# A decode kernel that streams its weights: half a row of w_q goes first, the keys second, and ACT's transfers begin behind a memset

## The chip, the cores and the metric

The kernel runs on one core of one Trainium2 chip. The metric is the device time of one execution in microseconds; the median of a few runs is given, with the lowest and the highest.

## The reference

One token (`x`, 576 numbers) goes through a sliding-window attention with cached keys and values and through a dense layer with gelu; a gate mixes the two.

```python
W = min(4096, max(256, Sk // 4))                      # the last 4096 positions of 32768
q = (x @ wq).reshape(B, Sq, Hq, Dh)                   # 32 query heads of 128
k = repeat(k_cache[:, :, Sk - W:, :], 2, axis=1)      # 16 heads of keys and values
v = repeat(v_cache[:, :, Sk - W:, :], 2, axis=1)
p = softmax(q . k * Dh ** -0.5)
a = (p . v).reshape(B, Sq, Hq * Dh) @ wo
b = gelu(x @ w1 + b1) @ w2 + b2                       # 576 -> 4608 -> 576
g = sigmoid((x * gate_w).sum(-1))
return g * a + (1 - g) * b
```

All arrays are bfloat16. Every byte of the windowed keys and values and of the weights is used once, which makes 53.6 MB to be read.

## The kernel before

**The order is written out by hand.** The kernel is under a manual schedule: each engine runs its instructions in the order in which the program states them. All large transfers are issued by SP in one queue of hardware DMA. ACT issues three small ones.

**The tiles.** Keys and values are loaded as eight tiles each of two heads (`load_kv`, its `dma_start` is line 102): 64 partitions for the one head, 64 for the other, and 16,384 bytes for each partition. Six buffers (`kv_pool`) hold them. `load_flat` (line 118, its `dma_start` is line 120) loads a flat stretch of w_q or w1 as 128 partitions; three buffers (`w_pool`) hold those. w_q comes as two tiles of 18,432 bytes per partition, `wq_t[0]` and `wq_t[1]`; a partition has four and a half rows of w_q, each 8,192 bytes long.

**The head of the program.** SP issues, in this order: the first keys (line 134), x9 (line 136, x as 64 x 9), the two w_q tiles, and the second keys (line 142). ACT issues x_row (line 130), gate_w (line 131) and b2 (line 132). b2 goes into row 0 of `b2_r`, a tile that GpSimd fills with zeros first (line 129), so its transfer waits for that memset; it is the third of ACT's, and b2 is used at the end of the kernel alone (line 679).

**What follows.** TensorE multiplies x9 with a selection matrix into `x_ps` (line 373); VectorE makes from it `x2`, the stationary operand of the w_q and w1 products (line 381). VectorE then multiplies x_row with gw_row (line 385), and TensorE spreads the sum over the partitions for the gate (line 390). Behind that product stand the transposes of the first two heads of keys (line 235, copied out by VectorE and ACT at lines 244 and 246), and then the 36 products with w_q (line 409), half of them on each tile of w_q. The scores (line 266) need q. A loop over the 16 heads then interleaves transposes, scores, the softmax of groups of four heads and the products with the values (line 342), with w1 placed among them (line 454). At the end come wo and w2 (line 671), the last quarter of w2 in three pieces (line 690), the copy of the result (line 703) and its transfer (line 704).

**Completion counters.** DMAs issued by SP and ACT take turns on eight completion counters. A DMA that takes a counter for the second time waits until the one that had it before has landed. In the built program before, the ninth DMA in this order is SP's third tile of keys, and it waits for one of ACT's small transfers.

Of the kernel before, what the change touches and what calls it, by code (L numbers as in the profile page):

```python
# [16 lines left out]
def kernel(  # L17
# [15 lines left out]
    nc = tc.nc  # L33
# [13 lines left out]
    NQ = 4  # L47
# [6 lines left out]
    NM = 9  # L54


    QC = Hq * Dh // 8
# [33 lines left out]
    wq_flat = A_wq.rearrange("a b -> (a b)").rearrange("(p n) -> p n", p=P)  # L91
# [7 lines left out]
    def load_kv(cache, m, name):  # L99
        t = kv_pool.tile([P, NCK, Dh], BF16, name=name, tag="kv")  # L100

        nc.sync.dma_start(  # L102
            out=t[:],
            in_=cache[0, 2 * m : 2 * m + 2, Sk - W : Sk, :].rearrange(
                "e (p c) d -> p e (c d)", c=NCK
            ),
        )
        return t

    def load_k(m):  # L110
        return load_kv(A_k_cache, m, "k_t")
# [3 lines left out]

    WMAX = 41 * 256

    def load_flat(src, lo, n, name):
        t = w_pool.tile([P, WMAX], BF16, name=name, tag="w")
        nc.sync.dma_start(out=t[:, 0:n], in_=src[:, lo : lo + n])  # L120
        return t

    k_tiles, v_tiles = {}, {}
# [3 lines left out]

    b2_r = const.tile([P, D], BF16, name="b2_r")
    nc.gpsimd.memset(b2_r[:], 0.0)
    nc.scalar.dma_start(out=x_row[:], in_=A_x.rearrange("a b d -> (a b) d"))  # L130
    nc.scalar.dma_start(out=gw_row[:], in_=gate_w.rearrange("(o n) -> o n", o=1))
    nc.scalar.dma_start(out=b2_r[0:1, :], in_=B_b2.rearrange("(o n) -> o n", o=1))

    k_tiles[0] = load_k(0)
    x9 = const.tile([P // 2, NM], BF16, name="x9")
    nc.sync.dma_start(out=x9[:], in_=A_x.rearrange("a b (i m) -> (a b i) m", m=NM))
    wq_t = []
    QP = 2 * NM
    for i in range(2):
        wq_t.append(load_flat(wq_flat, i * QP * QC, QP * QC, "wq_t"))  # L140

    k_tiles[1] = load_k(1)

# [12 lines left out]
        out=row_f[:], in_=ident_f[:, 0 : 32 * (NQ - 1) + 1 : 32], axis=AX.X, op=ALU.add  # L156
# [4 lines left out]
        out=dup[:].rearrange("k (i e) -> k i e", e=2),  # L161
        in_=ident[0 : P // 2, 0 : P // 2].rearrange("k (i e) -> k i e", e=1).to_broadcast(
            [P // 2, P // 2, 2]
        ),
    )
    par = const.tile([P, 2], FP32, name="par")
    for o in range(2):
        nc.vector.tensor_reduce(
            out=par[:, o : o + 1],
            in_=ident_f[:].rearrange("p (i o) -> p o i", o=2)[:, o, :],  # L170
# [7 lines left out]
        out=turn[:].rearrange("p j (h q) -> p j h q", h=OJ),  # L178
        in_=ident[:].rearrange("p (o q j) -> p j o q", o=1, j=OJ).to_broadcast(
            [P, OJ, OJ, P // OJ]  # L180
        ),
# [4 lines left out]
        out=m_r[:], in_=ident_f[:].rearrange("p (s r) -> p r s", r=R), axis=AX.X, op=ALU.add  # L186
# [5 lines left out]
        out=row_e[:], in_=ident_f[:].rearrange("p (a e q) -> p e a q", e=2, q=2), axis=AX.XY,  # L192
# [3 lines left out]
        out=row_e[:], in0=row_e[:], scalar1=-MASK, scalar2=MASK, op0=ALU.mult, op1=ALU.add  # L196
    )
    mask = const.tile([P, BC * P], BF16, name="mask")
    for e in range(2):
        nc.vector.tensor_copy(  # L200
            out=mask[:, e::2], in_=row_e[:, e : e + 1].to_broadcast([P, BC * P // 2])
# [4 lines left out]
        out=m_c[:], in_=ident_f[:].rearrange("p (t c r) -> p c t r", c=BC, r=R), axis=AX.XY,  # L206
# [4 lines left out]
        out=m_hl[:], in_=ident_f[:].rearrange("p (h q) -> p h q", h=OJ), axis=AX.X, op=ALU.add  # L211
# [10 lines left out]
    for dst, src in ((sel, ident), (sel_f, ident_f)):  # L222
        nc.vector.tensor_copy(
            out=dst[:].rearrange("p l (o h) -> p l o h", o=2),
            in_=src[:].rearrange("p (h l x) -> p l x h", h=2, l=2)[:, :, 0:2, :],
# [149 lines left out]
    for dst, src, s in (  # L375
# [10 lines left out]
        out=junk[:], in0=x_row[:], in1=gw_row[:], scale=1.0, scalar=0.0,  # L386
# [11 lines left out]
        out=omg[:], in0=g_t[:], scalar1=-1.0, scalar2=1.0, op0=ALU.mult, op1=ALU.add  # L398
# [7 lines left out]
    for b in range(NM * NQ):  # L406
        m, t = b // NQ, b % NQ
# [22 lines left out]
    for m in range(HB // 2):  # L430
        lo = R * (NGR - 1) + RP * m
        nc.vector.tensor_copy(  # L432
            out=qz[:, m :: HB // 2, lo : lo + RP],
            in_=qT[:, :, m, :].rearrange("p i b -> p b i"),
# [7 lines left out]
    def w1_load(i):  # L442
        return load_flat(w1_flat, i * W1N, W1N, "w1_t")
# [105 lines left out]
    for h in range(NU):  # L549
# [4 lines left out]
        if h == 1:  # L554

            for o in range(2):
                nc.sync.dma_start(
                    out=b1_r[o : o + 32 * (NQ - 1) + 1 : 32],
                    in_=B_b1.rearrange("(o t k n) -> o t k n", o=2, t=NQ, k=2)[o],
# [57 lines left out]
    for i in range(NOG // 2):  # L617
        t = w_pool.tile([P, WMAX], BF16, name="wo_t", tag="w")
        nc.sync.dma_start(
            out=t[:, 0 : 2 * OJ * D].rearrange("p (o n) -> p o n", o=2),  # L620
            in_=wo_view[:, 2 * i : 2 * i + 2, :],
# [3 lines left out]
    for g in range(NG):  # L625
        t = kv_pool.tile([P, NCK * Dh], BF16, name="w2_t", tag="kv")
# [7 lines left out]
        out=ot[:], in0=o_sb[:], scalar=g_t[:, 0:1], in1=r_sums[:], op0=ALU.mult, op1=ALU.mult  # L634
# [3 lines left out]
    for j in range(OJ):  # L638
# [3 lines left out]
        out=ow_m[:],  # L642
# [5 lines left out]
    with nc.allow_low_precision("one of the eight summands is not zero"):  # L648
        nc.vector.tensor_reduce(  # L649
            out=ow[:].rearrange("p j o -> p (j o)"), in_=ow_m[:], axis=AX.X, op=ALU.add  # L650
# [17 lines left out]
    for n, four in enumerate(blocks):  # L668
# [11 lines left out]
        out=part_s[:], in0=b2_r[:].rearrange("p (k n) -> p k n", k=2), scalar=omg[:, 0:1],  # L680
# [16 lines left out]
    for j in range(RJ):  # L697
# [7 lines left out]
        out=out.rearrange("a b (t n) -> (a b t) n", t=NQ), in_=y[0 : 32 * (NQ - 1) + 1 : 32, :]  # L705
# [31 lines left out]
```

## Time and profile before

| | |
|---|---|
| time, median of 3 runs | 134.98 us (134.93 to 135.19) |
| time of the profiled execution | 134.92 us |
| its span, first to last instruction | 133.0 us |
| PE busy | 90.9 us (68%) |
| DVE busy | 61.3 us (46%) |
| ACT busy | 48.5 us (36%) |
| POOL busy | 4.2 us (3%) |
| DMA packets, bytes | 4553 packets, 53.79 MB, mean 404 GB/s |

The profiled execution's time is 1.92 us longer than its span: what lies around the first and the last instruction. Times in the views are microseconds from the first instruction; in a timeline row come start, duration, engine, line, operation and, in brackets, how long the engine sat idle before it and what ended that. "SPq" and "ACTq" are the engines' queues issuing DMAs, and the duration is that of the issue, not of the transfer. A stretch of time lists its ends and its length, then for each engine its busy time and its number of instructions (PE, weight loads, DVE, ACT, POOL), then TensorE's granted clock, the share of the 16 DMA engines that was busy, and the bytes of the packets that start in it, as GB/s.

### The profile page before, as it was taken

Reading aid. Unit: us, or ns where it says so; the run is one execution under the profiler, and the core shown is the slowest. Engines: PE = TensorE matmul, PEld = TensorE weight load, DVE = VectorE, ACT = ScalarE, POOL = GpSimd, SP = SyncE. Lnnn points to the kernel's source line nnn. Section 1 sums busy time; section 2 is a strip of 40 time slices with the busy share of each in tenths; the row PEclk is TensorE's granted clock in tenths of the full one; section 3 lists DMA queues with packets and bytes.
Section 4 is the critical chain, followed back from the end, with each engine's and each line's share of the span. In section 5 each row is a group of like instructions: output and inputs, shape, how many; then the busy total and the mean of one; then the engine's idle time right before and its main releaser. Section 6 shows DMA issues by size and latency. Waiting matters only on the chain.

```text
span 133.0 us, 2659 instructions
## 1 busy us (share of the span) xinstructions
PE 90.9 (68%) x1127; PEld 58.6 (44%) x1127; DVE 61.3 (46%) x165; ACT 48.5 (36%) x91; POOL 4.2 (3%) x11
## 2 busy tenths in 40 slices
PE   0007985299296899969076996978988648459660
PEld 0007741267174565645045654645655215135340
DVE  4964632035227665575004257564866463440020
ACT  3003750066336787757001153766584100000000
POOL 8400000000000000000000000000000000000000
PEclk9999999757999999999955559999999955555865
DMA  3999999999999999999899999999999999999960
GB/s 79 400 430 432 443 424 429 434 436 412 431 458 399 453 414 446 409 421 479 379 453 409 448 414 443 419 439 424 434 429 429 415 418 430 436 424 415 428 261 0
DMA packets 4553, 53.79 MB, mean 404 GB/s; under 512 B 563, under 2 KB 702, under 8 KB 1214
## 3 DMA queue, kind: packets, MB, share of 16 engines
q1 hardware_dynamic: 4536, 53.62, 95.2%
q8 instruction: 9, 0.15, 0.4%
q14 instruction: 2, 0.02, 0.0%
q10 hardware_dynamic: 6, 0.00, 0.0%
HBM read 53.62 MB, written 0.00 MB: 403 GB/s over the span
## 4 chain that ended last, share of the span: by engine, by line
DMA 58%; PE 28%; DVE 8%; SPq 2%; issue 2%; DVEq 0%
DMA w_t<-in_B_w_dram 41%; DMA k_t<-in_A_k_cache_dram 17%; PE tp L235 13%; PE s_ps L266 4%; PE acc L342 3%; DVE kT L244 3%; PE h_ps L454 2%; PE hT L481 2%; DVE a_s L358 2%; PE y_ps L690 1%; SPq L120 1%; SPq L102 1%; DVE ez L320 1%; DVE part_s L679 1%; DVE h_r L472 1%
## 5 line engine op out<-in xcount | busy, mean ns | idle before, releaser
L246 ACT CAST kT<-tp 128x512 bf16<-128x512 f32 x80 | 44.1, 586 | 44.2 <-PE tp L235 43.7
L244 DVE CAST kT<-tp 128x512 bf16<-128x512 f32 x48 | 33.0, 690 | 38.6 <-PE tp L235 34.1
L235 PE MATMUL tp<-ident,k_t 128*128 128x128 bf16 x512 | 45.5, 238 | 4.7 <-DMA k_t<-in_A_k_cache_dram 3.0
L235 PEld LDWEIGHTS <-k_t 128*128 128x128 bf16 x512 | 35.2, 107 | 17.4 <-issue 12.8
L342 PE MATMUL acc<-v_t,ez 128*32 128x512 bf16 x128 | 13.3, 459 | 2.2 <-DVE a_s L358 1.9
L266 PE MATMUL s_ps<-kT,qz 128*32 128x512 bf16 x128 | 13.5, 416 | 0.3 <-DVE qz L432 0.3
L454 PE MATMUL h_ps<-w_t,x 128*32 128x288 bf16 x72 | 4.0, 365 | 6.8 <-DMA w_t<-in_B_w_dram 6.8
L454 PEld LDWEIGHTS <-x 128*32 128x32 bf16 x72 | 2.8, 117 | 7.6 <-issue 7.1
L373 PE MATMUL x_ps<-x,dup 64*128 64x9 bf16 x1 | 0.2, 163 | 8.8 <-DMA x<-in_A_x_dram 8.8
L342 PEld LDWEIGHTS <-ez 128*32 128x32 bf16 x128 | 3.7, 102 | 5.5 <-issue 3.1
L266 PEld LDWEIGHTS <-qz 128*32 128x32 bf16 x128 | 3.3, 94 | 3.8 <-issue 0.8
L679 DVE SCALAR_TENSOR_TENSOR part_s<-b_r,omg,part 128x576 f32<-128x576 bf16 x1 | 0.8, 814 | 8.8 <-PE part L671 8.8
L671 PE MATMUL part<-wo_t,ow 128*1 128x288 bf16 x64 | 4.0, 443 | 1.0 <-DVE ow L649 1.0
L671 PE MATMUL part<-w_t,gt 128*1 128x288 bf16 x54 | 3.7, 364 | 1.4 <-DMA w_t<-in_B_w_dram 1.4
L358 DVE SCALAR_TENSOR_TENSOR a_s<-acc,m_c,a_s 128x128 f32<-128x128 f32 x12 | 4.2, 351 | 0.4
L307 ACT ACTIVATE pr<-ms,nb 128x512 bf16<-128x512 f32 x4 | 2.9, 722 | 4.1 <-DVE nb L304 4.1
L320 DVE COPY ez<-pT 128x64 bf16<-128x64 bf16 x32 | 3.6, 183 | 1.7 <-PE pT L315 1.5
L148 DVE CAST ident_f<-ident 128x128 f32<-128x128 bf16 x1 | 3.0, 3000 | 1.8 <-POOL ident masks.py:199 1.8
L365 PE MATMUL o_ps<-m_r,a_s 128*128 128x8 f32 x8 | 1.9, 315 | 2.8 <-DVE a_s L358 2.8
L365 PEld LDWEIGHTS o_ps<-m_r,a_s 128*128 128x128 f32 x8 | 1.6, 249 | 4.9 <-DVE a_s L358 2.5
L671 PEld LDWEIGHTS <-gt 128*1 128x1 bf16 x54 | 2.2, 104 | 2.9 <-issue 2.0
L481 PE MATMUL hT<-sel_f,h_r 128*64 128x4 f32 x36 | 2.7, 264 | 1.2 <-DVE h_r L472 1.2
(82 smaller groups left out, 48.2 us busy)
## 6 DMA issues: line engine op xcount, KB each, us to landing
k_t<-in_A_k_cache_dram SPq DMA_DIRECT2D x8, 2048.0 KB, 27.5
v_t<-in_A_v_cache_dram SPq DMA_DIRECT2D x8, 2048.0 KB, 24.5
w_t<-in_B_w_dram SPq DMA_DIRECT2D x2, 2592.0 KB
wq_t<-in_A_wq_dram SPq DMA_DIRECT2D x2, 2304.0 KB, 14.4
wo_t<-in_A_wo_dram SPq DMA_DIRECT2D x2, 2304.0 KB
w_t<-in_B_w_dram SPq DMA_DIRECT2D x2, 1296.0 KB, 21.6
w_t<-in_B_w_dram SPq DMA_DIRECT2D x1, 864.0 KB
w_t<-in_B_w_dram SPq DMA_DIRECT2D x1, 720.0 KB, 21.3
```

Of the source, the lines that this page charges most:

```text
L148: nc.vector.tensor_copy(out=ident_f[:], in_=ident[:])
L235: nc.tensor.matmul(tp[:, c * P : (c + 1) * P], lhsT=k_tiles[h // 2][:, (h % 2) * NCH + i * BC + c, :], rhs=ident[:], start=True, stop=True,)
L244: nc.vector.tensor_copy(out=dst, in_=tp[:])
L246: nc.scalar.copy(out=dst, in_=tp[:])
L266: nc.tensor.matmul(s_tiles[b][32 * t : 32 * (t + 1), :], lhsT=qz[:, h // 2, lo : lo + 32], rhs=kT[h][:, i * BC * P : (i + 1) * BC * P], st ...
L320: nc.vector.tensor_copy(out=ez[:, b % 2, m, NQ * s : NQ * (s + 1), :, RP * m : RP * (m + 1)], in_=pT[:].rearrange("p c (t s r) -> p t c s ...
L342: nc.tensor.matmul(acc[b][32 * ct : 32 * ct + 4 * R, :, :], lhsT=ez[:, b % 2, ul // 2, n, :, :].rearrange("p c r -> p (c r)"), rhs=v_tiles ...
L358: nc.vector.scalar_tensor_tensor(out=a_s[:], in0=acc[b][:, c, :], scalar=m_c[:, c : c + 1], in1=a_s[:], op0=ALU.mult, op1=ALU.add,)
L365: nc.tensor.matmul(o_ps[:], lhsT=a_s[:], rhs=m_r[:], start=True, stop=True)
L454: nc.tensor.matmul(h_box[0][32 * t : 32 * (t + 1), k, 0:FB], lhsT=x2[:, m, :], rhs=w[:, off : off + FB], start=(m == 0), stop=(m == NM - 1),)
L481: nc.tensor.matmul(box[0][64 * e : 64 * (e + 1), j, :], lhsT=rows[:, j : j + RJ * 63 + 1 : RJ], rhs=sel_f[:, e, :], start=True, stop=True,)
L671: nc.tensor.matmul(part[32 * t : 32 * t + 1, k, 0:DB], lhsT=col, rhs=w[:, i * D + k * DB : i * D + (k + 1) * DB], start=(n == 0), stop=(n ...
```

## The change

`load_flat` gets cuts: a stretch may come in several transfers, and a function given as `between` is called after the first. The first tile of w_q is cut after 2,048 elements, so its first transfer is 4,096 bytes for each of 128 partitions, half a row of w_q. It becomes the first transfer that SP issues; then come the first keys and x9, then the other 14,336 bytes per partition of the same tile, the second w_q tile and the second keys, as before. SP issues one DMA more.

On ACT, b2's transfer, which waits for the memset of `b2_r`, moves from the third place to the first; x_row and gate_w follow it.

In the built program the ninth DMA in the order of the completion counters is now SP's second tile of keys, and it waits for b2's. No instruction of PE, DVE or POOL is added, removed or moved.

```diff
-    def load_flat(src, lo, n, name):
+    def load_flat(src, lo, n, name, cuts=(), between=None):
         t = w_pool.tile([P, WMAX], BF16, name=name, tag="w")
-        nc.sync.dma_start(out=t[:, 0:n], in_=src[:, lo : lo + n])
+        edges = (0, *cuts, n)
+        for i, (a, b) in enumerate(zip(edges, edges[1:])):
+            if i == 1 and between is not None:
+                between()
+            nc.sync.dma_start(out=t[:, a:b], in_=src[:, lo + a : lo + b])
         return t
...
     nc.gpsimd.memset(b2_r[:], 0.0)
+    nc.scalar.dma_start(out=b2_r[0:1, :], in_=B_b2.rearrange("(o n) -> o n", o=1))
     nc.scalar.dma_start(out=x_row[:], in_=A_x.rearrange("a b d -> (a b) d"))
     nc.scalar.dma_start(out=gw_row[:], in_=gate_w.rearrange("(o n) -> o n", o=1))
-    nc.scalar.dma_start(out=b2_r[0:1, :], in_=B_b2.rearrange("(o n) -> o n", o=1))
-
-    k_tiles[0] = load_k(0)
     x9 = const.tile([P // 2, NM], BF16, name="x9")
-    nc.sync.dma_start(out=x9[:], in_=A_x.rearrange("a b (i m) -> (a b i) m", m=NM))
-    wq_t = []
+
+    def first_keys():
+        k_tiles[0] = load_k(0)
+        nc.sync.dma_start(out=x9[:], in_=A_x.rearrange("a b (i m) -> (a b i) m", m=NM))
+
     QP = 2 * NM
-    for i in range(2):
-        wq_t.append(load_flat(wq_flat, i * QP * QC, QP * QC, "wq_t"))
+    wq_t = [
+        load_flat(wq_flat, 0, QP * QC, "wq_t", (NQ * QC,), first_keys),
+        load_flat(wq_flat, QP * QC, QP * QC, "wq_t"),
+    ]
```

## The prediction

> **What bounds the kernel now.** I read the page's slices first, then the chain that ended last, then stretches of the DMA stream, and last the first five microseconds instruction by instruction.
>
> ```profile
> DMA  3999999999999999999899999999999999999960
> GB/s 79 400 430 432 443 424 429 434 436 412 431 458 399 453 414 446 409 421 479 379 453 409 448 414 443 419 439 424 434 429 429 415 418 430 436 424 415 428 261 0
> HBM read 53.62 MB, written 0.00 MB: 403 GB/s over the span
> DMA 58%; PE 28%; DVE 8%; SPq 2%; issue 2%; DVEq 0%
> ```
>
> The DMA engines are busy nine tenths or more in every slice but the first, one in the middle and the last two. The chain is 58% DMA, and where it runs over PE the slices still show the DMA full. So the kernel is one stream of 53.62 MB with a head before it and a tail behind it.
>
> ```profile
> 104.13 22.33 DMA w_t<-in_B_w_dram
> 126.46 0.04 issue
> 126.50 0.55 PE part L671 x9
> ...
> 127.95 1.98 PE y_ps L690 x44
> 129.93 0.02 issue
> 129.95 0.31 DVE y L703
> 4.00:128.00 124.00, 88.98 (x1087) 57.47 (x1091) 58.81 (x164) 47.25 (x90) 0.76 (x2) 0.85 1.01 427
> ```
>
> The chain in order of time: a piece of w2, issued 22 us earlier, lands at 126.46, and what follows it takes the rest of the span of 133.0 us. The last row is a stretch from 4 to 128 us: its last two columns say that the DMA share was 1.01 and the rate 427 GB/s, or 26.7 GB/s for each of the 16 DMA engines. A change that neither removes bytes nor changes that rate can move the end only by moving the start of the stream. The transfer that ends the chain waits 22 us behind others, so SP's later issues have far more slack than anything discussed here.
>
> Now the head. First the timeline (start, duration; ACTq, SPq are issues of DMAs):
>
> ```profile
> 0.73 0.50 ACTq L130 DMA_DIRECT2D x_row<-in_A_x_dram  x1
> 0.73 0.58 POOL L129 MEMSET b_r<- 128x576 bf16 x1 [0.29 <-POOLq L721]
> 0.73 0.66 SPq L102 DMA_DIRECT2D k_t<-in_A_k_cache_dram  x1
> 1.26 0.21 ACTq L131 DMA_DIRECT2D gw_row<-in_gate_w_dram  x1
> 1.44 0.58 SPq L136 DMA_DIRECT2D x<-in_A_x_dram  x1
> 1.51 0.44 ACTq L132 DMA_DIRECT2D b_r<-in_B_b_dram  x1
> 2.07 1.26 SPq L120 DMA_DIRECT2D wq_t<-in_A_wq_dram  x2
> ```
>
> Then stretches of the same microseconds; the last column counts the bytes of packets that start in the stretch:
>
> ```profile
> 2.10:2.30 0.20, 0.00 (x0) 0.00 (x0) 0.20 (x1) 0.20 (x1) 0.20 (x2) 1.00 3.62 655
> 2.30:2.70 0.40, 0.00 (x0) 0.00 (x0) 0.40 (x1) 0.40 (x1) 0.40 (x2) 1.00 0.00 0
> 2.70:2.90 0.20, 0.00 (x0) 0.00 (x0) 0.20 (x1) 0.20 (x1) 0.20 (x1) 1.00 1.81 655
> 2.90:3.50 0.60, 0.00 (x0) 0.00 (x0) 0.60 (x1) 0.36 (x1) 0.60 (x1) 1.00 0.00 0
> 3.50:3.82 0.32, 0.00 (x0) 0.00 (x0) 0.32 (x1) 0.00 (x0) 0.32 (x1) 1.00 2.16 819
> ```
>
> 655 GB/s for 0.20 us is 131 KB, eight rows of 16,384 bytes: eight engines take up the first keys at 2.1 to 2.3, the other eight only at 2.7 to 2.9. The tile is loaded as two heads of 64 partitions each, and eight and eight fits those halves. Then nothing starts until 3.50 to 3.82, when 819 GB/s x 0.32 us = 262 KB, all sixteen second rows, begin. At 26.7 GB/s a row takes 0.61 us. Sixteen engines that begin row two at 3.6 on average stand where they would have stood had they all run at full rate from 3.6 - 0.61 = 3.0. I call that the stream's true start: 3.0, which is 2.26 us after SP began to issue the first transfer at 0.73. During about 0.8 of this (2.2 to 3.0) at least half of the engines already hold a row and run below rate.
>
> **The change, part by part.** *The block.* 128 x 4096 bytes = 0.524 MB at 427 GB/s occupies the stream for 1.23 us. It is taken out of the first w_q transfer, so the total stays. The block adds one row per partition, which is eight more packets on each engine; they are priced below with the pieces of w2.
>
> Its gain follows from two bounds. Let the block's true start be s, and let i be what its issue takes on SP. The keys' issue then begins at 0.73 + i + 0.05, and their own true start is 2.26 us later at the latest, if nothing of their start improves: 3.04 + i. They begin to flow when both the block is through (s + 1.23) and they are ready. The stream before had its true start at 3.0, and with the block ahead that same point is 4.23. So the gain is the smaller of 3.0 - s and 4.23 - (3.04 + i) = 1.19 - i.
>
> For i, plain issues late in the kernel and the first keys themselves are the ends:
>
> ```profile
> 9.89 0.43 SPq L120 DMA_DIRECT2D w_t<-in_B_w_dram  x1
> 103.75 0.33 SPq L629
> 125.08 0.53 PE L671 MATMUL part<-w_t,gt 128*1 128x288 bf16 x9 [0.54 <-DMA w_t<-in_B_w_dram]
> 126.50 0.54 PE L671 MATMUL part<-w_t,gt 128*1 128x288 bf16 x9 [0.90 <-DMA w_t<-in_B_w_dram]
> ```
>
> A one-level block of w1 was issued in 0.43 us, one of w2 in 0.33, the keys in 0.66. So i is 0.33 to 0.66 and the second bound is 0.53 to 0.86. I take i = 0.5, nearer to 0.43 because the form is L120's, raised because it is the program's first issue: 0.69.
>
> For s no row shows a one-level block that starts on idle engines. From above: it could start as the keys did, s = 3.0, gain nothing. From below: all sixteen engines begin together as early as the first eight did after their issue (2.1 less the issue's end 1.39 = 0.75 us) behind an issue of 0.33, s = 1.8, gain 1.2. I take 2.3: the time at which the first eight engines had their row, since the half-and-half start goes with the two-level shape and the block has one level. That bounds the gain at 0.7. Both bounds agree on about 0.7; less 0.1 for the packets, **0.6 us**.
>
> A rule speaks against cutting off so small a transfer. The Trainium skill, "DMA: Bandwidth & Descriptors", section "Rules for kernel authors", asks for 128 partitions and at least 1 MiB per DMA for full bandwidth; its section "Anatomy of one DMA" gives about 2.0 us + bytes / 436 GB/s (for the path through GpSimd), an estimate of 3.2 us for this block instead of 1.23, by which the cut would bring nothing. Inside the stream the trace does not agree: the two rows above are waits for pieces of w2 that landed 1.42 us apart, and the second piece is 128 x 2304 x 2 bytes = 0.59 MB, so it ran at 415 GB/s. That is 0.04 us longer than at 427, for eight short rows on each engine; so I take under 0.1 us for the block's eight packets. On idle engines the rule may hold; that is the second rival.
>
> *ACT's transfers.* b2 moves ahead of x_row and gw_row and waits for the memset (0.73 + 0.58 = 1.31), so ACT issues nothing before that. Queued behind that wait on ACT are x_row, gw_row and the table load. The three issues take 0.50 + 0.21 + 0.44 = 1.15 us, so they end at 1.31 + 1.15 = 2.5 instead of 1.95. It frees the first 0.6 us for SP alone: a gain somewhere between nothing and the 0.33 us by which the keys' 0.66 exceeds the fastest plain issue, which I count inside i. The Trainium skill, same page, section "Issuing engines are not separate DMA queues", says that issuing from several engines only saves sequencer time; by it this part would be worth nothing.
>
> *What is late.* x9 and the first keys now stand behind 1.23 us more of stream, which starts 0.6 earlier: about 0.6 later in all.
>
> ```profile
> 8.80 0.16 PE L373 MATMUL x_ps<-x,dup 64*128 64x9 bf16 x1 [8.80 <-DMA x<-in_A_x_dram]
> 9.61 0.74 DVE L385 CUSTOM_DVE_ANT_0 junk<-x_row,gw_row 1x576 bf16<-1x576 bf16 x1
> 10.98 1.46 PE L235 MATMUL tp<-ident,k_t 128*128 128x128 bf16 x12
> 17.86 1.26 PE L409 MATMUL q_ps<-wq_t,x 128*32 128x512 bf16 x18
> 19.57 1.26 PE L409 MATMUL q_ps<-wq_t,x 128*32 128x512 bf16 x18 [0.46 <-DMA wq_t<-in_A_wq_dram]
> 25.75 1.46 PE L235 MATMUL tp<-ident,k_t 128*128 128x128 bf16 x12 [3.00 <-DMA k_t<-in_A_k_cache_dram]
> ```
>
> PE starts at 9.4 instead of 8.80, its transposes at 11.6 instead of 10.98. The second w_q tile lands 0.6 earlier, so the 0.46 wait disappears and PE's own lateness leads: q ends some 0.2 later. The second keys, 0.6 earlier, cut the 3.00 wait to about 2.2. That wait is the cover; PE is late nowhere after 25. Without it, PE would carry its 0.6 on, and it still would not reach the end while the stream's 22 us queue stands. gw_row is now issued by 2.5 and needed at 10.2 (9.61 + 0.6): 7.7 us against 8.35 before.
>
> *SP's order.* One DMA more makes SP's second keys the ninth, and in the built program they wait for b2's completion; all of SP's later issues stand behind it. Block, first keys and w_q are 0.52 + 2.10 + 1.84 + 2.36 = 6.8 MB, 16 us of queued work, so b2 may land as late as 15 us and cost nothing.
>
> **Sum.** 134.92 us of the profiled execution (133.0 of span, 1.92 around it) less 0.6 is 134.3; the median of the runs, 134.98, lies 0.06 higher, so I name 134.4. A measurement of this kernel can tell about 0.2%, 0.27 us: faster means below 134.7, slower above 135.25.
>
> **The rivals.** *More is won:* part of the keys' 2.26 us passes while the block flows, and the block's issue takes 0.33. Then s = 1.8 to 1.9 alone decides, gain 1.1, 133.9. For it: eight engines had their keys only 0.75 us after the issue. Against it: all sixteen then ran below rate until 3.5, and nothing shows that this depends on the shape.
>
> *The start belongs to whatever comes first:* the block shows the same 2.26 us, s = 3.0 less at most the shorter issue. Gain 0 to 0.3, less the packets: 134.7 to 135.0, no change. For it: both halves of the keys finished row one together at 3.5 to 3.8 though they began 0.6 apart, as if something common opened at about 2.9. Against it: eight engines and eight engines fit the shape.
>
> *Slower:* ACT's issues, moved to 1.31 to 2.5, now fall on the first keys' issue at 1.3 to 1.9 instead of lying beside a transfer with nothing ahead of it. If the two queues' descriptors are worked one after another, the keys are ready up to 1.15 us later than 3.54, at 4.7. It decides from 4.23 on: the engines run dry between the block and the keys, and the end comes 0.3 to 0.5 later, with the packets 135.3 to 135.5. For it: SP's issues beside ACT's took 0.58 and 0.66, alone later 0.33 and 0.43. Against it: the same line, L102, alone later, still takes 0.54 to 0.59,
>
> ```profile
> 10.37 0.59 SPq L102 DMA_DIRECT2D k_t<-in_A_k_cache_dram  x1
> ...
> 34.11 0.54 SPq L102
> ```
>
> so little of the 0.66 is ACT's doing.
>
> **How the numbers follow.** Forecast, gain 0.4 to 0.85 (134.1 to 134.6), with 0.1 of scatter either way: 0.55. More is won: 0.13. Start belongs to the first: 0.20. Slower: 0.12. So faster 0.68, same 0.20, slower 0.12. The range 134.0 to 135.1 leaves out the slower case and half of the case above the forecast, 0.18 in all. The forecast's own range is 134.0 to 134.7.
>
> **What would show it.** Right: SP's first issue takes 0.5 or less; rows of 4,096 bytes start on all sixteen engines within 0.2 us near 2.0, so the slice from 0 to 3.3 us moves clearly more than 79 GB/s; no stretch without new packets between block and keys; x_ps starts near 9.4, the wait for the second keys near 2.2, and the last w2 landing near 125.9 instead of 126.46. Wrong: a gap in packet starts of over 0.6 us behind the block (third rival), a block whose engines begin eight and eight or stall to 2.9 (second), or an end that does not move although the stream starts earlier.

## The result and the profile after

| | before | changed |
|---|---|---|
| median of 22 runs each | 135.04 us (134.84 to 135.32) | 134.56 us (134.41 to 136.28) |
| profiled execution, span | 134.92 us, 133.0 us | 134.47 us, 132.6 us |

The ratio is 0.9972, with a 95% interval from 0.9959 to 0.9985: 0.38 us faster, somewhere between 0.2 and 0.55. Of the changed kernel's 22 runs, 20 lie between 134.41 and 134.76, one at 135.05 and one at 136.28. A ratio here leaves out runs more than 1.5% above the fastest of their kernel (with the block alone, six of twelve), so for a kernel whose times spread widely the median and the range say more than the ratio.

The same three lines of the page as before:

```profile
DMA  4999999999999999999999999999999999999960
GB/s 111 453 419 447 434 417 440 420 441 438 414 435 425 430 420 438 420 439 433 411 450 415 445 410 435 435 415 445 410 450 420 412 431 428 428 428 419 419 243 5
HBM read 53.62 MB, written 0.00 MB: 405 GB/s over the span
```

The bytes are the same. Only the first two slices carry clearly more (111 and 453 GB/s instead of 79 and 400). The head of the timeline shows why:

```profile
0.73 0.38 SPq L124 DMA_DIRECT2D wq_t<-in_A_wq_dram  x1
1.17 0.63 SPq L102 DMA_DIRECT2D k_t<-in_A_k_cache_dram  x1
1.34 0.51 ACTq L135 DMA_DIRECT2D b_r<-in_B_b_dram  x1
```

The block was issued in 0.38 us, where the keys had taken 0.66. ACT's first issue begins at 1.34, behind the memset. Stretches of the same time (last column: GB/s of packets that start in the stretch):

```profile
1.60:2.00 0.40, 0.00 (x0) 0.00 (x0) 0.16 (x1) 0.00 (x0) 0.40 (x2) 1.00 0.97 113
2.00:2.40 0.40, 0.00 (x0) 0.00 (x0) 0.40 (x1) 0.00 (x0) 0.40 (x2) 1.00 0.23 61
2.40:2.80 0.40, 0.00 (x0) 0.00 (x0) 0.40 (x1) 0.29 (x1) 0.40 (x2) 1.00 0.94 276
2.80:3.20 0.40, 0.00 (x0) 0.00 (x0) 0.40 (x1) 0.40 (x1) 0.40 (x1) 1.00 0.92 369
3.20:3.60 0.40, 0.00 (x0) 0.00 (x0) 0.40 (x1) 0.40 (x1) 0.40 (x1) 1.00 1.29 522
3.40:3.80 0.40, 0.00 (x0) 0.00 (x0) 0.40 (x1) 0.39 (x1) 0.40 (x1) 1.00 1.49 614
```

Eleven rows (113 GB/s x 0.40 us = 45 KB) have been taken up by 2.0, where before no row had been. They were slow: in the trace's packet records these eleven took 0.19 to 0.81 us each, where most rows of this length took 0.16. Rows then flow from about 2.4, and no stretch is empty up to the keys, whose 16 KB rows begin at 3.4 to 3.8 (614 GB/s; the last two stretches overlap).

The true start, as the prediction defines it, can be worked out for any kernel. Each packet that begins before 7 us is charged bytes / 26.85 GB/s + 0.008 us, about what a row took at full rate (0.61 us for 16,384 bytes, 0.16 for 4,096); one still under way at 7 is charged in proportion. The sum, divided by the 16 engines, is taken from 7. It gives 3.04 before and 2.44 now: 0.60 us earlier. Time that engines lose between their start and 7 us is in this figure too. On PE:

```profile
9.52 0.17 PE L384 MATMUL x_ps<-x,dup 64*128 64x9 bf16 x1 [9.52 <-DMA x<-in_A_x_dram]
18.59 2.13 PE L420 MATMUL q_ps<-wq_t,x 128*32 128x512 bf16 x36
25.12 0.84 PE L246 MATMUL tp<-ident,k_t 128*128 128x128 bf16 x12 [2.47 <-DMA k_t<-in_A_k_cache_dram]
```

x9 is 0.72 us later, the products with w_q run as one group without a wait, and the second keys end their wait at 25.12 instead of 25.75. The tail, from the timeline and the chain of waits:

```profile
126.08 0.54 PE L682 MATMUL part<-w_t,gt 128*1 128x288 bf16 x9 [0.85 <-DMA w_t<-in_B_w_dram]
129.55 0.31 DVE L714 CAST y<-y_ps 128x144 bf16<-128x144 f32 x1 [2.08 <-PE y_ps L701]
```
```profile
105.99 22.10 DMA w_t<-in_B_w_dram
...
128.13 1.40 PE y_ps L701 x35
```

The w2 piece that ended PE's wait at 126.50 now ends it at 126.08. The stream still queues for 22 us ahead of the last transfer on the chain. Of the 0.63 us at 25 us, 0.42 is left at 126, and the copy of the result begins at 129.55 instead of 129.95, 0.40 earlier.

### The profile page after: what moved, and what is told of

Same layout as the page of the kernel before. It is cut to its first block, busy times and chain, and to the rows that moved or that the text cites. A ratio compares the mean times of both kernels' runs of the same rounds, so it can differ in the third digit from the quotient of the medians.

```text
span 132.6 us, 2660 instructions
## 1 busy us (share of the span) xinstructions
PE 90.9 (69%) x1127; PEld 58.2 (44%) x1127; DVE 61.3 (46%) x165; ACT 48.8 (37%) x91; POOL 4.2 (3%) x11
## 4 chain that ended last, share of the span: by engine, by line
DMA 60%; PE 28%; DVE 8%; issue 1%; SPq 0%; DVEq 0%
DMA w_t<-in_B_w_dram 42%; DMA k_t<-in_A_k_cache_dram 16%; PE tp L246 13%; PE s_ps L277 4%; PE acc L353 4%; DMA wq_t<-in_A_wq_dram 3%; DVE kT L255 3%; PE h_ps L465 2%; PE hT L492 2%; DVE a_s L369 2%; PE y_ps L701 1%; DVE ms L296 1%; DVE ez L331 1%; DVE h_r L483 1%; PE o_ps L376 0%
## 5 line engine op out<-in xcount | busy, mean ns | idle before, releaser
L246 PE MATMUL tp<-ident,k_t 128*128 128x128 bf16 x512 | 46.1, 240 | 3.9 <-DMA k_t<-in_A_k_cache_dram 2.5
L465 PE MATMUL h_ps<-w_t,x 128*32 128x288 bf16 x72 | 5.0, 433 | 6.4 <-DMA w_t<-in_B_w_dram 6.4
L465 PEld LDWEIGHTS <-x 128*32 128x32 bf16 x72 | 3.4, 135 | 7.5 <-issue 6.7
L682 PE MATMUL part<-wo_t,ow 128*1 128x288 bf16 x64 | 3.5, 402 | 1.0 <-DVE ow L660 1.0
L682 PE MATMUL part<-w_t,gt 128*1 128x288 bf16 x54 | 2.9, 285 | 1.8 <-DMA w_t<-in_B_w_dram 1.7
L303 PE MATMUL mT<-ident_f,mx 128*1 128x128 f32 x4 | 1.1, 270 | 3.3 <-DVE mx L296 3.3
```

The lines of the kernel that those rows point to most:

```text
L246: nc.tensor.matmul(tp[:, c * P : (c + 1) * P], lhsT=k_tiles[h // 2][:, (h % 2) * NCH + i * BC + c, :], rhs=ident[:], start=True, stop=True,)
L465: nc.tensor.matmul(h_box[0][32 * t : 32 * (t + 1), k, 0:FB], lhsT=x2[:, m, :], rhs=w[:, off : off + FB], start=(m == 0), stop=(m == NM - 1),)
L682: nc.tensor.matmul(part[32 * t : 32 * t + 1, k, 0:DB], lhsT=col, rhs=w[:, i * D + k * DB : i * D + (k + 1) * DB], start=(n == 0), stop=(n ...
```

## The experiments

Each ran beside the kernel before. "Start" is the true start worked out as above, from one profiled execution each. The starts of "block only" and "second keys at 5 us" come from executions of 137.11 and 137.16 us and hold what engines lost by 7 us.

| kernel | start | median, range of runs | ratio to before |
|---|---|---|---|
| before | 3.04 | 135.04 (134.84 to 135.32) | 1 |
| the change | 2.44 | 134.56 (134.41 to 136.28) | 0.9972 [0.9959, 0.9985] |
| block only | 3.09 | 136.33 (134.45 to 137.37) | 0.9999 [0.9978, 1.002] |
| ACT's order only | 2.82 | 134.93 (134.70 to 135.22) | 0.9991 [0.9983, 1.0] |
| plain block, 16 KB rows | 2.47 | 134.58 (134.34 to 134.85) | 0.9967 [0.9955, 0.9979] |
| keys first, 4 KB rows | 3.29 | 135.78 (135.63 to 136.01) | 1.0057 [1.0045, 1.0069] |
| nothing on ACT | 2.54 | 134.63 (134.49 to 134.75) | 0.9965 [0.9953, 0.9978] |
| block only, a second time | 2.47 | 134.58 (134.30 to 136.62) | 0.9967 [0.9949, 0.9986] |
| ACT held by x_row | 2.54 | 134.63 (134.48 to 134.69) | 0.9963 [0.995, 0.9976] |
| block of 2 KB rows | 2.91 | 136.29 (134.73 to 137.47) | 1.0039 [1.0005, 1.0073] |
| w_q block in two levels | 2.98 | 135.16 (135.01 to 135.39) | 1.0004 [0.9995, 1.0013] |
| block of every second partition | 2.97 | 134.94 (134.87 to 135.72) | 0.9993 [0.998, 1.0007] |
| keys by head | 2.85 | 134.91 (134.69 to 135.22) | 0.9989 [0.9979, 0.9999] |
| ACT not held, second keys at 5 us | 2.82 | 136.83 (135.47 to 138.05) | 1.0095 [1.0063, 1.0127] |

### The two halves of the change, each alone

*Block only:* the changed kernel with ACT's old order.

```diff
-    nc.scalar.dma_start(out=b2_r[0:1, :], ...)
     nc.scalar.dma_start(out=x_row[:], ...)
     nc.scalar.dma_start(out=gw_row[:], ...)
+    nc.scalar.dma_start(out=b2_r[0:1, :], ...)
```

> The block of 4,096-byte rows goes first, ACT's three transfers keep the order of before (x_row, gate_w, b2, no wait ahead of them). Theory S (the gain is the early start of the block, 2.44 instead of 3.04, and ACT's order is nothing): rows of the block flow from about 2.4 on as in the changed kernel, the time is 0.3 to 0.5 us below before. Rival A (ACT's transfers beside SP's first issue are what delays the first start): SP's first issue takes 0.5 to 0.66 us again, the first rows stall till 2.7 or later, less than 0.15 us is left of the gain.

SP's first issue again took 0.38 us, so ACT's concurrency isn't in it; rival A falls on that count. The fastest run, 134.45, has the whole gain, but the twelve runs spread over 3 us, ten of them lie above 135, and their median is 1.24 us above before. So theory S, by which ACT's order is nothing, doesn't hold for these runs. The same program did better a second time, below.

*ACT's order only:* the kernel before, with ACT's lines of the change.

> The keys go first as before, only ACT's order is that of the change. Theory S: SP's first issue keeps 0.54 us or more, the second rows of the first keys begin at 3.3 to 3.8 as before, the time is within 0.15 us of before. Rival A: the first issue falls below 0.5 us, the first rows flow 0.3 us earlier or more, and most of the gain of 0.4 us is there.

The first issue took 0.65 us, the time is 0.12 us below before and the interval touches 1. The start in the trace is 0.2 earlier (2.82), more than Theory S had expected, but little of it reaches the time.

### What makes the block start early

*Plain block with the keys' row length:* the cut is at 8,192 elements.

```diff
-        load_flat(wq_flat, 0, QP * QC, "wq_t", (NQ * QC,), first_keys),
+        load_flat(wq_flat, 0, QP * QC, "wq_t", (4 * NQ * QC,), first_keys),
```

> As the changed kernel, but the block has 16,384 bytes per partition, the same row length as the keys, in one level of 128 partitions. Theory S (it is the form: a block of one level starts on all 16 engines at once): all 16 engines take their first row at 1.75 to 2.2, their second rows begin at about 3.0, true start 2.4 to 2.5, time 0.4 us below before. Rival L (it is the row length: long rows are slow to start): the first rows take 1.3 us or more, second rows begin at 3.3 or later, true start 2.7 to 3.0, gain 0 to 0.25 us. x9 and the keys land 3.7 us later than in the changed kernel; both theories expect that the end does not feel it.

Start 2.47, ratio 0.9967: row length isn't it, and a longer block costs nothing, although x9 came to PE at 13.22.

*Keys first in short rows:* the kernel before with ACT's new order, the first keys cut at 4,096 bytes per partition.

```diff
...
+    keys = A_k_cache[0, 0:2, Sk - W : Sk, :].rearrange("e (p c) d -> p e (c d)", c=NCK)
+    for a, b in ((0, 16), (16, NCK)):
+        nc.sync.dma_start(out=t[:, a:b, :], in_=keys[:, :, a * Dh : b * Dh])
```

> The keys go first in two transfers, 4,096 bytes per partition (two levels, two heads of 64 partitions) and then the other 12,288; w_q is uncut; ACT's order is that of the change. Theory S: eight engines take rows at about 2.1, the other eight 0.5 us later, true start 2.8 to 3.0, gain at most 0.2 us. Rival L: all engines run by 2.5, true start 2.4 to 2.5, gain 0.3 to 0.5 us, as much as with the block of w_q.

0.57% slower than before, worse than either theory had. Start 3.29; short rows of the keys don't help. The start explains 0.25 us of the 0.77. The trace records sixteen landings for each large transfer, as many as there are engines, and they are taken here as one for each engine. Eight engines had the first piece of the keys by 4.65 us, the other eight from 5.07 on. The last landing of the last w2 piece, which the end waits for, is 0.98 us later than before (130.55 instead of 129.57), the mean of the sixteen 0.54. So uneven engines are part of it; why they start unevenly stays open.

*The same block of w_q, read in two levels as the keys are:*

```diff
+            rows = src[:, lo + a : lo + b]
+            if i == 0 and between is not None:
+                rows = rows.rearrange("(e p) n -> p e n", e=2)
...
```

> As the changed kernel, the same 4,096 bytes per partition of w_q first, but read in two levels like the keys: partition 2p+e takes row 64e+p of the block (so that part of q is computed from permuted weights; no other work changes). Theory S (the two-level form is what starts late): eight engines take rows at about 2.15 instead of 1.75, the others about 0.5 us after, the block is through 0.4 us later, the gain falls to 0.1 us or below. Rival D (it is the keys' own place in memory, or being the first transfer): as the changed kernel, 134.5.

This is the cleanest pair: same bytes, same tile, same place in the order as in the changed kernel; only which row goes to which partition differs. Its issue and its first stretches:

```profile
0.73 0.65 SPq L127 DMA_DIRECT2D wq_t<-in_A_wq_dram  x1
```
```profile
1.60:2.00 0.40, 0.00 (x0) 0.00 (x0) 0.16 (x1) 0.00 (x0) 0.40 (x2) 1.00 0.00 0
2.00:2.40 0.40, 0.00 (x0) 0.00 (x0) 0.40 (x1) 0.00 (x0) 0.40 (x2) 1.00 1.04 123
2.40:2.80 0.40, 0.00 (x0) 0.00 (x0) 0.40 (x1) 0.17 (x1) 0.40 (x2) 1.00 0.24 51
2.80:3.20 0.40, 0.00 (x0) 0.00 (x0) 0.40 (x1) 0.40 (x1) 0.40 (x1) 1.00 0.71 195
```

The issue is back at 0.65 us, nothing starts before 2.0, and by 3.2 it has begun 0.15 MB where the changed kernel had begun 0.33 MB (the last columns x 0.40 us). The gain is gone: 1.0004. Theory S's verdict holds, the form of the first transfer decides; the rows were not taken eight and eight, though (123 GB/s x 0.40 us is twelve rows).

*Half the rows, twice as long, every second partition:*

```diff
+    HC = 2 * NQ * QC
...
+    nc.sync.dma_start(out=w0[0::2, 0:HC], in_=wq_flat[0::2, 0:HC])
+    first_keys()
+    nc.sync.dma_start(out=w0[1::2, 0:HC], in_=wq_flat[1::2, 0:HC])
+    nc.sync.dma_start(out=w0[:, HC : QP * QC], in_=wq_flat[:, HC : QP * QC])
...
```

> As the changed kernel, but the block has the same 0.52 MB as 64 rows of 8,192 bytes, every second partition, one level. Theory G (rows are handed to the engines at a pace of about 128 in 0.7 us, which is why the block's rows flow only from about 2.4 though the first is taken at 1.75): 64 rows are handed out by 2.1, the true start is 2.1 to 2.2, and the time 0.2 to 0.3 us below the changed kernel's, 134.3. Rival O (something opens at about 2.4 whatever waits): as the changed kernel, 134.6. Rival P (every second partition shares the way into the memory and runs at half rate): the block takes 2.4 us instead of 1.2, and the time is that of before or above.

```profile
0.73 0.59 SPq L150 DMA_DIRECT2D wq_t<-in_A_wq_dram  x1
```

None of the three. The issue took 0.59 us although the block has one level, the first rows came at 2.1, the start is 2.97. Fewer rows did not start earlier, 0.88 us passed from the first row to the start (G falls), and nothing opened at 2.4 (O falls). Once they flowed, rows of 8 KB took the normal 0.31 us (P falls).

*Keys by head:* the first keys as two transfers of 64 partitions, with ACT's new order.

```diff
...
+    for e in range(2):
+        nc.sync.dma_start(out=t[e::2, :, :],
+            in_=A_k_cache[0, e, Sk - W : Sk, :].rearrange("(p c) d -> p (c d)", c=NCK))
```

> The keys go first as before and ACT's order is that of the change, but the first keys come as two transfers of one level, one head of 64 partitions each (every second partition). Theory S: the first rows are taken at 1.75 to 1.9 instead of 2.16, the true start is 2.3 to 2.5 and the gain 0.3 to 0.5 us, without a block of w_q. Rival D: the first rows at 2.16 and second rows at 3.3 to 3.8 as before, no gain. Rival P: the first rows early, but 16 KB rows at 1.2 us each, no gain or a loss.

First rows at 2.12, start 2.85, like ACT's order alone (2.82). So one level isn't sufficient. Of the first transfers tried, only those over all 128 partitions with one level on both sides were issued in 0.37 to 0.39 us and had rows at 1.75; every other form took 0.59 to 0.66 and had them at 2.09 to 2.18.

### Whether the block covers the keys' start

*Block of 2 KB rows:* the cut is at 1,024 elements.

> As the changed kernel, with a block of 2,048 bytes per partition, half as long: it covers 0.6 us. If the keys need their 2.26 us from the start of their issue at 1.17, they flow from 3.43 only, the block is through at about 3.1, and the gain falls from 0.4 to about 0.1 to 0.2 us. If the keys' start passes behind any block, the gain stays 0.4 us (134.5) and no stretch is empty behind the block.

One stretch, first of this kernel, then of the changed one:

```profile
3.40:3.80 0.40, 0.00 (x0) 0.00 (x0) 0.40 (x1) 0.39 (x1) 0.40 (x1) 1.00 0.00 0
```
```profile
3.40:3.80 0.40, 0.00 (x0) 0.00 (x0) 0.40 (x1) 0.39 (x1) 0.40 (x1) 1.00 1.49 614
```

With the short block no packet starts for 0.4 us: the engines hold first rows of keys that aren't through, just as at 2.9 to 3.5 in the kernel before. The start is 2.91. The keys' 2.26 us from their issue at 1.17 ask for 3.43, less the block's 0.67 (0.61 for its bytes, 0.06 for its packets), which is 2.76. So the start-up is paid by the keys wherever they stand, and 4 KB of block hide it. The times, however, were not 0.1 to 0.2 us below before; they spread from 134.73 to 137.47, nine of the twelve above 135, although ACT was held.

### What ACT's order is for

*Nothing on ACT:* SP issues x_row and gate_w behind x9, b2 behind w_q.

> As the changed kernel, but ACT issues no transfer: SP issues x_row and gate_w behind x9, and b2 behind w_q. The second keys wait for the block. Theory A2 (a small transfer that ACT issues together with SP's first one upsets the start, and holding ACT back is what takes that away): all runs lie within 0.3 us of each other, near 134.5; no row of the first keys takes over 0.9 us. Theory K (it is the second keys' early issue, at 3.67, that upsets it, and in the changed kernel these wait for b2): the same here, since the second keys wait for the block until about 4.1. Theory S alone (ACT's order is nothing): 134.5 as well.

*Block only, a second time:* the block first in the program's order, ACT's three transfers after it with the old order. This was to deal the counters otherwise.

> The block goes first, ACT's transfers are in the old order with no wait ahead, but the counters are dealt so that the second keys wait for the block (about 4.1) instead of x_row (2.0). Theory A2: the times spread over 2 us or more as in the run with the block alone (134.45 to 137.37). Theory K: they lie within 0.4 us of each other, near 134.6.

The edit moved lines of the source and nothing else. The built program is that of "block only": the same instructions in the same order on every engine, on the same counters, and the issues stand within 0.01 us of those in the other trace. So it tells nothing of theory K. It is twelve more runs of one program, on another chip.

*ACT held, b2 on SP behind the second keys:*

```diff
+    nc.gpsimd.memset(x_row[:], 0.0)
     nc.scalar.dma_start(out=x_row[:], ...)
...
     k_tiles[1] = load_k(1)
+    nc.sync.dma_start(out=b2_r[0:1, :], ...)
```

> The block goes first, ACT begins behind a memset (of x_row), but SP issues b2 behind the second keys, so these wait for nothing and are issued at about 3.7. Theory A2: steady, near 134.5. Theory K: the times spread over 2 us or more.

With nothing on ACT, and with ACT held by another memset, the five runs of each lie within 0.3 us, at the changed kernel's time. With the block alone, this time, nine of twelve lie at 134.3 to 134.8 and three from 135.0 to 136.6. The first time it had been two and ten. In the two traces of that one program x9 comes to PE at

```profile
12.14 0.16 PE L384 MATMUL x_ps<-x,dup 64*128 64x9 bf16 x1 [12.14 <-DMA x<-in_A_x_dram]
```
```profile
9.53 0.17 PE L384 MATMUL x_ps<-x,dup 64*128 64x9 bf16 x1 [9.53 <-DMA x<-in_A_x_dram]
```

in the run of 137.11 and in the one of 134.58. So the program alone does not decide whether it happens, nor, by these counts, how often. At three in twelve, ten steady runs would come by chance about once in eighteen (0.75 to the tenth), so the two steady kernels beside it are weak evidence for holding ACT.

With ACT held and b2 behind them, the second keys went out at 4.05 and not at about 3.7, so that run doesn't test theory K either. The issue times of the kernels so far fitted theory K (spread at 3.67 to 3.73, steady at 4.05 or later). One run was left for that:

*ACT not held, second keys at 5 us:*

```diff
     nc.scalar.dma_start(out=x_row[:], ...)          # at once, no memset ahead
     nc.scalar.dma_start(out=gw_row[:], ...)
...
+    nc.gpsimd.memset(b2_r[:], 0.0)                  # the last of POOL's memsets
+    nc.sync.dma_start(out=b2_r[0:1, :], ...)
+    k_tiles[1] = load_k(1)
```

> The block goes first, ACT issues x_row and gate_w at once with no wait ahead; SP issues b2 and then the second keys only behind a memset that ends at about 4.8. What it tells apart: in the three kernels whose times spread over 2 us the second keys were issued at 3.67 to 3.73, in the steady ones with a block at 4.05 or later, though ACT was held in one of the spread ones and not in two. Theory K (the second keys issued at 3.7, while the block and the first keys are still at their start, upset it): here they are issued at about 5, so the times lie within 0.4 us of each other, near 134.6. Theory A2 (ACT's transfer beside SP's first one does it): the times spread over 2 us again, 134.4 to 137.

```profile
0.73 0.52 ACTq L134 DMA_DIRECT2D x_row<-in_A_x_dram  x1
0.73 0.39 SPq L124 DMA_DIRECT2D wq_t<-in_A_wq_dram  x1
5.15 1.22 SPq L102 DMA_DIRECT2D k_t<-in_A_k_cache_dram  x2
...
12.23 0.16 PE L384 MATMUL x_ps<-x,dup 64*128 64x9 bf16 x1 [12.23 <-DMA x<-in_A_x_dram]
```

Theory K falls: the second keys went out at 5.15, and yet all eight runs are above 135.4 and spread to 138. The timeline says where it happens. x9 arrives at 12.23 instead of 9.52, though it stands behind the same bytes. By the landings, fourteen engines had the first keys by 9.8 and two only at 11.84 and 12.01. Two stay behind to the end of the stream: the mean landing of the last w2 piece is 0.26 us later than before, the last landing 2.30 later. The page's GB/s line begins like this in the run with the block alone, and in this one:

```profile
GB/s 164 336 367 435 426 427 428 441 420 439 422 446 417 431 431 414 436 433 439 408 442 431 421 436 417 441 426 436 421 417 424 421 417 436 428 430 418 380 99 0
```
```profile
GB/s 140 394 376 436 432 417 443 417 439 440 422 426 431 422 436 419 436 433 436 426 418 436 426 431 422 426 446 417 431 412 431 410 431 431 428 424 415 383 69 0
```

The start is early (164 and 140 against 111), and the two slices behind it lose more than that (336, 367 and 394, 376 against 453, 419). These runs go with theory A2: with the plain block first and a small transfer that ACT issues in the same moment as SP's first, 21 of 32 runs lie above 135; with ACT held or idle and a block of 4 KB or more, 2 of 37. But it isn't shown as the cause. The kernel before issues the same pair at once and is steady, the 2 KB block spreads with ACT held, and one program gave ten of twelve once and three of twelve another time. Neither theory fits every kernel: A2 misses the 2 KB block, K misses this one. What the engines do in that time the trace doesn't name; it stays open.

## Why the prediction was right, and where it was not

The forecast, 134.4 us, and its mechanism were right: the end moves with the stream's start. Step by step:

- **The bound.** Right. The products with w_q and the wait for the second keys took up PE's lateness: x9 at 9.52 (forecast 9.4), the wait 2.47 us (forecast 2.2). Even x9 at 13.22, with the 16 KB block, did not reach the end. One detail was off: the products with w_q, now one group from 18.59, end at 20.72, 0.11 earlier than before and not 0.2 later.
- **The issue, i.** Taken as 0.5, measured 0.38, so the keys' bound on the gain is 1.19 - 0.38 = 0.81 and does not decide.
- **The block's start, s.** Taken as 2.3, measured 2.44. That term alone set the gain: 3.04 - 2.44 = 0.60, from which the block's packets take their share (under 0.1, as forecast; by the charge of 0.008 us for each of eight, an estimate of 0.06). The sign named for it did not come: rows did not start on all sixteen engines within 0.2 us, eleven were up by 2.0 and the rest flowed from 2.4. That 2.3 came so near is in part luck, since its reason was half wrong (below).
- **The rivals on the start.** For the start that belongs to whatever comes first, the block would have shown 2.26 us from its issue; it took 1.71 (2.44 - 0.73), and in two levels 2.25. For more to be won, s had to be 1.8 to 1.9.
- **The cover.** Right: 1.23 us of block leave no empty stretch, 0.6 us of block leave one of 0.4 us.
- **The reason for the early start.** Only half right. The form decides, as the two-level block showed. But "eight and eight fits those halves" was wrong: the source alternates the heads' partitions (2p+e), so the heads are no halves, and a form of one level over every second partition started as late as the keys. By the traces the 0.60 us is made up of an issue 0.28 shorter (0.38 instead of 0.66), 0.13 less from its end to the first row (0.64 instead of 0.77) and 0.19 less from there to the true start (0.69 instead of 0.88).
- **ACT's transfers.** Wrong in kind. They were priced inside i, as time that SP's first issue would get back. That issue took 0.37 to 0.39 us with ACT held, not held, or without transfers. The order goes with steadier times, but not as a shown cause: with the block alone the medians were 136.33 and, the second time, 134.58, where the changed kernel had 134.56. The sentence of the Trainium skill weighed there ("DMA: Bandwidth & Descriptors", "Issuing engines are not separate DMA queues") agrees with the medians of the steady kernels: 134.63 without transfers on ACT, 134.56 with. It doesn't speak of the spread.
- **The rule against small transfers** (the Trainium skill, same page, "Rules for kernel authors"). The block on idle engines did take long to complete; the chain of waits charges it 3.71 us:

```profile
0.73 3.71 DMA wq_t<-in_A_wq_dram
4.46 20.61 DMA k_t<-in_A_k_cache_dram
```

  The fit of the Trainium skill (same page, "Anatomy of one DMA"), weighed in the prediction, gave an estimate of 3.2. But the keys flow right behind it, so the fixed part costs no stream time. By that the rule doesn't decide here.
- **SP's order.** The second row shows a slip in the description of the change and in the prediction: the second keys wait for the block, which has their counter in the built program, and not for b2. They went out at 4.46 instead of 3.37. It cost nothing that shows: these keys still ended their wait 0.63 us earlier.
- **The loss on the way.** The sum let 0.6 us of start arrive whole at the end. 0.63 arrived at 25 us and 0.40 at the copy of the result; the medians differ by 0.48, the ratio says 0.38. The landings of the last w2 piece show where the rest went: their mean moved from 128.90 to 128.32, 0.58 earlier, the last of them from 129.57 to 129.17, 0.40 earlier. So nearly all of the start arrived in the mean of the engines, but the end waits for the last engine, which was 0.67 behind the mean before and 0.85 behind it now. This is one execution each.
- **The slower rival.** Its mechanism, ACT's issues delaying the keys' issue, did not come about: the keys' issue took 0.63 us and no stretch was empty.

## What to carry to other kernels

When a kernel is one saturated stream, its first transfer's start-up is idle time at the head, and a plain block over all 128 partitions, placed ahead of a transfer that is slow to start, can hide part of it if its own bytes last as long as that start-up. Size it by the empty stretch behind it: here 2 KB per partition left a hole, and 16 KB cost nothing, since PE's lateness did not reach the end. Expect the end to follow the last engine and not the mean. Repeat such a change often enough to see the spread, on more than one occasion: the block alone looked like a loss once and like the whole gain the next time. And look in the built program whether an experiment changed what it was to change; one here did not.

## What the runs showed of the hardware that was not expected

- A first transfer was issued in 0.37 to 0.39 us when it was 128 partitions in one level, and in 0.59 to 0.66 us in any other form tried; its first rows were taken up at 1.75 and at 2.09 to 2.18.
- Some time more passed between the first row taken up and the true start: 0.64 to 0.88 us in ten of the fourteen traces (1.75 to 2.44 with the block, 2.17 to 2.98 in two levels). It was more with short rows of the keys, with the 2 KB block, and in the traces of 137.11 and 137.16 us.
- In two kernels with a block ahead and small transfers on the other queue beside the first issue, some engines had the first keys up to 3 us after the others, without any difference in SP's own issue time, and were still behind at the end (last landing 131.93 and 131.87 us, mean 129.52 and 129.16). One of these programs ran without it in another trace. The cause isn't shown.
